# Block-masked attention and two MLPs: the score products of two heads side by side on 64 rows each

## The chip, the cores and the metric

The kernel runs on one core of one Trainium2 chip. The metric is the device time of one execution in microseconds (us), as the median of several runs. The profile is that of one further execution. Engines are named as in the profile: PE (matrix products), PEld (loading the stationary operand), DVE, ACT, POOL (elementwise engines), SP (the queue that issues all transfers here).

## The reference

```python
# q, k, v: (batch 4, heads 8, sequence 576, head_dim 64), float32
scores = scale * np.matmul(q, k.transpose(0, 1, 3, 2))
mask = block_i >= block_j                 # blocks of 64 positions
scores = np.where(mask, scores, -1000000000.0)
attn = np.exp(scores - max); attn = attn / (sum(attn) + 1e-09)
x = np.matmul(attn, v)                    # to (2304 tokens, 512)
h = x @ w_in;  g = h * np.cos(h);        x = g @ w_out      # MLP 1, width 2048
h = x @ w_in2; r = np.maximum(h, 0.0);   x = (r * r) @ w_out2   # MLP 2
```

MLP 1's weights come in as float64, all else as float32.

## The kernel before, in words

**Work and order.** The heads are taken in pairs, whose 2 x 64 dimensions fill the 128 partitions (TOP is the first head, BOT the second). Attention runs in 20 units: units 0 to 3 are batch 0, first 256 rows, for the four pairs; units 4 to 7 are batch 0, the other 320 rows; units 8 to 19 are whole pairs of batches 1 to 3. The first half of MLP 1 runs between them, group by group: tiles `h` (x times w_in) and `y` (times w_out). From about 400 us on only MLP work is left.

**The planner.** Nothing is issued as it is written. `Recorder` notes each operation with an estimated cost, the tiles it needs and a rank (its place in the list plus an offset per kind and phase, `PUT_OFF`, L36), and `schedule` then makes the order of every engine from these. Some copies may go to one of two engines by choice. Eight PSUM banks are shared by kind: `h` may hold 6, `y` 3, scores `s` 5, transposes `t` 3, products with v `a` 1, and one of each kind is kept free for it (`BANKS`, L22).

**Precision.** A float32 operand is split into a high and a low part (fp32r), and a product is three products: high by high, high by low, low by high.

**One unit, before.** `prep` (L856) transposes k and q of the pair on PE and makes the parts kh, kl (keys) and sa, sb (queries, scaled). From unit 4 on (`u.apart` false), the parts of one head are laid over both halves of the partitions: sa holds head 0's high part on its own half and its low part on the other half, sb the same for head 1. To match, six transfers through SP copy the halves of kh twice into ka and kb, and kl into the buffers kz, whose other half is zero (`both`, L866). Then two products over 128 rows, with ka and with kz, give the sum of the three. Units 0 to 3 do without copies: three products over the 64 rows of a head.

`unit_scores` (L926) runs per head and group of rows: rows 0 and 1 of 128 in one bank (128 and 256 keys), then row 3 (512 keys) and row 2 (384); a unit "P" computes the last 64 rows of both heads at once from `tails`. After the products come per row: `soft_min` on DVE (mask and row minimum), the exponential on ACT with its sum, the small add of 1e-9 (`eps`) and the reciprocal for the whole group, and the scaling on POOL (`times`). `unit_transpose` (L992) turns the result by PE and copies it out; `unit_av` (L1024) multiplies with v for one head. In units 0 to 7 (`u.plain`) v stays float32 and gives 64 output columns; from unit 8 on v's two parts fill 128 columns.

**Order in the list.** In the second part: head 0 row 3, head 0 row 2, P, product with v of head 0, `prep` of the next unit, head 1 row 3, row 2, product with v of head 1 (`UNITS` L1057, `attention` L1080).

Of the kernel before, what the change touches and what calls it, by code (L numbers as in the profile page):

```python
# [30 lines left out]
APART = 4  # L31
E1 = 7
# [313 lines left out]
def kernel(  # L346
# [264 lines left out]
    for i in range(2):  # L611
        sa = T(sb, [128, 512], F32R, f"sa{i}")
        sb_ = T(sb, [128, 512], F32R, f"sb{i}")
        tails = [T(sb, [128, 128], F32R, f"tail{i}{j}") for j in "hl"]
        for t in tails:
            memset(f(t), 0.0)

        pads = [T(sb, [128, 576], F32R, f"kz{i}{j}") for j in "ab"]
        memset(f(pads[0][64:128]), 0.0)
        memset(f(pads[1][0:64]), 0.0)  # L620
        QS.append((sa, sb_, tails, pads))
# [193 lines left out]
    def load_pair(b, p, part):  # L815
# [3 lines left out]
        u.apart = part == 1 or len(units) < APART  # L819
# [36 lines left out]
    def prep(u):  # L856

        kn, qn, vn = u.nat
        sa, sb_, tails, pads = u.S = QS[u.i % 2]
        ka, kb, kl, kh = u.K = tuple(T(sb, [128, 576], F32R, n, 2) for n in ("ka", "kb", "kl", "kh"))  # L860
# [5 lines left out]
        def both(which):  # L866
            if u.apart:
                return
            for i, h in enumerate((TOP, BOT)):
                if which == "h":  # L870
                    for g in (TOP, BOT):
                        dma(f(u.K[i][g]), f(kh[h]), 147456, 600.0)
                else:
                    dma(f(pads[i][h]), f(kl[h]), 147456, 600.0)

        def queries(t, c):
            if u.apart:

                act(sa[:, c], t, ACTF.Copy, scale=scale)
                stt(sb_[:, c], t, scale, f(sa[:, c]), ALU.mult, ALU.subtract)  # L880
                return
# [13 lines left out]
        else:  # L895
# [7 lines left out]
            both("h")  # L903
            lo_part(kl[:, 512:576], t[:, 0:64], kh[:, 512:576])
            both("l")
# [19 lines left out]
    @of("scores")  # L925
    def unit_scores(u, kind):  # L926

        e = T(sb, [128, 576], F32, "e", E1)
        st = T(sb, [128, 8], F32, "st", 6)
        if kind == "P":  # L930
            for j in range(2):
                t = bank("s")
                kc = slice(j * 288, j * 288 + 288)
                (th, tl), kl, kh = u.S[2], u.K[2][:, kc], u.K[3][:, kc]
                for i, (l, r) in enumerate(((th, kh), (th, kl), (tl, kh))):
                    matmul(t[:, 0:288], l, r, i == 0, i == 2, holds=(e, st))
                soft_min(e[:, kc], t[:, 0:288], mask[:, 0:288], st[:, 2 + j:3 + j])
            tt(st[:, 0:1], st[:, 2:3], st[:, 3:4], ALU.min)
            parts = [(0, 576)]
        else:  # L940
            h, ts_ = kind
            half = (TOP, BOT)[h]
            t = bank("s")
            parts, o = [], 0
            for j in ts_:
                n = 128 * (j + 1)
                c = slice(j * 128, j * 128 + 128)
                if u.apart:

                    (qh, ql), (kl, kh) = [x[half, c] for x in u.S[:2]], [x[half, 0:n] for x in u.K[2:]]  # L950
                    for i, (l, r) in enumerate(((qh, kh), (qh, kl), (ql, kh))):
                        matmul(t[:, o:o + n], l, r, i == 0, i == 2, holds=(e, st))
                else:

                    matmul(t[:, o:o + n], u.S[h][:, c], u.K[h][:, 0:n], True, False, holds=(e, st))
                    matmul(t[:, o:o + n], u.S[h][:, c], u.S[3][h][:, 0:n], False, True)
                parts.append((o, n))
                o += n
            for i, (o, n) in enumerate(parts):
                soft_min(e[:, o:o + n], t[:, o:o + n], mask[:, 512 - n:512], st[:, i:i + 1])  # L960
        for i, (o, n) in enumerate(parts):
            x = e[:, o:o + n]
            turn("exp", x, x, ACTF.Exp, bias=st[:, i:i + 1], scale=-1.0, accum_out=st[:, 4 + i:5 + i])
        m = len(parts)
        sums = st[:, 4:4 + m]
# [8 lines left out]
        rs = st[:, 6:6 + m]  # L974
        dve(75, lambda: nc.vector.reciprocal(real(rs), real(st[:, 4:4 + m])), [rs], [st[:, 4:4 + m]])  # L975
        for i, (o, n) in enumerate(parts):
            times(e[:, o:o + n], e[:, o:o + n], st[:, 6 + i:7 + i])
        return e

# [10 lines left out]

    @of("weighted")
    def unit_transpose(u, kind, e):  # L992

        names = "h" if u.plain else "hl"
        if kind == "P" or kind[1][0] > 0:
            if not hasattr(u, "r2"):
                u.r2 = [T(sb, [128, 2, 4, 320], F32R, f"r2{i}") for i in names]
                u.r2t = T(sb, [128, 2, 64], F32R, "r2t")
        t = t_tile()
        if kind == "P":  # L1000
            for kt in range(4):
                transpose(t[:, kt * 128:kt * 128 + 128], e[:, kt * 128:kt * 128 + 128], holds=u.r2)
            src = t.rearrange("p (k h c) -> p h k c", k=4, h=2)
            parts_of(u, src, [r[:, :, :, 256:320] for r in u.r2])
            t2 = t_tile()
            transpose(t2[0:64, 0:128], e[:, 512:576], holds=[u.r2t])
            parts_of(u, t2[0:64, 0:128].rearrange("p (h c) -> p h c", h=2), [u.r2t[0:64], u.r2t[64:128]])
            return
        h, ts_ = kind
        if ts_[0] == 0:  # L1010
            u.r1 = [T(sb, [128, 384], F32R, f"r1{i}", 2) for i in names]
            for o in (0, 128, 256):
                transpose(t[:, o:o + 128], e[:, o:o + 128], holds=u.r1)
            parts_of(u, t[:, 0:384], u.r1)
            return
        n = ts_[0] + 1
        for kt in range(n):
            transpose(t[:, kt * 128:kt * 128 + 128], e[:, kt * 128:kt * 128 + 128], holds=u.r2)
        o = (ts_[0] - 2) * 128
# [4 lines left out]
    def unit_av(u, h, region):  # L1024
# [4 lines left out]
        if region == 1:  # L1029
            mms = [(0, 256, 0, [r[:, 0:256] for r in u.r1]), (128, 256, 1, [r[:, 256:384] for r in u.r1])]  # L1030
        else:
            mms = []
            for kt in range(4):
                c = 128 if kt == 3 else 0
                mms.append((c, 320, kt, [r[:, h, kt, c:320] for r in u.r2]))

            mms.append((256, 320, 4, [u.r2t[:, h, :]]))
        mine, other = (TOP, BOT) if h == 0 else (BOT, TOP)
        mms = [(c0, c1, kt, r) for c0, c1, kt, rs in mms for r in rs]
        xb = None if u.plain else T(sb2, [128, 320], F32, "xb", 2)  # L1040
# [337 lines left out]
```

## Time and profile before

| | |
|---|---|
| Median of 3 runs | 1052.7 us (1052.44 to 1053.11) |
| Profiled execution, its own time | 1059.5 us |
| Its span, first to last instruction | 1057.7 us |
| Mean granted TensorE clock | 0.995 of full speed |
| PE busy | 1020.6 us |
| DVE, ACT, POOL busy | 698.7, 676.7, 376.7 us |
| Moved by DMA | 129.16 MB |

A matrix product's busy time in the profile includes its way through the array, so products overlap in it and a busy PE need not be a full one. What a product takes of PE in a dense run is the distance from its start to the next start.

### The profile page before, as it was taken

The numbers are of one execution on the slowest core, as the hardware profiler recorded it, in microseconds if no ns is written. First come the engines' busy times: TensorE is split into PE (matmuls) and PEld (weight loads), VectorE is DVE, ScalarE is ACT, GpSimd is POOL, SyncE is SP. The second block draws the span as 40 slices with busy tenths as digits, with TensorE's granted clock in tenths as the row PEclk, the third lists the DMA queues.
The fourth block names the chain that finished last, engine by engine and source line by source line (L and its number), as shares of the span: only waits on it lengthen the run. The fifth ranks groups of instructions, "written<-read, shape, count | busy, mean of one in ns | idle before, by whom it ended". The sixth has DMA issues, their size and how long they took to land.

```text
span 1057.7 us, 18891 instructions
## 1 busy us (share of the span) xinstructions
PE 1020.6 (96%) x6440; PEld 926.8 (88%) x6440; DVE 698.7 (66%) x1805; ACT 676.7 (64%) x1685; POOL 376.7 (36%) x466
## 2 busy tenths in 40 slices
PE   8959999999999999999999999999999999999998
PEld 5657788889899989999889999988989888988987
DVE  4687499886758674567653326999877287747433
ACT  5688689888979886776574336777755364524312
POOL 5336224454545556948982222114120002000000
PEclk9989999999999999999999999999999999999999
DMA  6686534534425124455321223375761383131121
GB/s 156 160 187 165 140 93 120 140 81 119 114 72 126 43 64 136 136 167 189 113 86 63 90 71 119 115 226 156 266 197 53 120 321 98 60 100 51 60 70 40
DMA packets 125919, 129.16 MB, mean 122 GB/s; under 512 B 72832, under 2 KB 99456, under 8 KB 124800
## 3 DMA queue, kind: packets, MB, share of 16 engines
q1 hardware_dynamic: 125824, 127.96, 41.2%
q8 instruction: 51, 0.84, 0.3%
q14 instruction: 44, 0.36, 0.1%
HBM read 81.79 MB, written 31.98 MB: 108 GB/s over the span
## 4 chain that ended last, share of the span: by engine, by line
PE 58%; ACT 12%; DVE 12%; POOL 9%; DMA 5%; issue 4%; SPq 0%; ACTq 0%; DVEq 0%; POOLq 0%
PE y L512 24%; PE h L512 23%; PE a L512 4%; PE t L521 3%; ACT e L397 3%; PE s L512 3%; POOL gl L450 3%; POOL c L691 2%; POOL w L450 2%; DVE e L918 1%; DVE c L413 1%; POOL xl L450 1%; ACT r2h L465 1%; DVE r L406 1%; DVE gl L454 1%
## 5 line engine op out<-in xcount | busy, mean ns | idle before, releaser
L512 PE MATMUL h<-xh,w 128*128 128x256 f32 (+1 forms) x1408 | 288.6, 298 | 0.6 <-ACT u L465 0.4
L512 PEld LDWEIGHTS h<-xh,w 128*128 128x128 f32 x1408 | 231.1, 188 | 4.2 <-ACT u L465 0.9
L512 PE MATMUL y<-gh,w 128*128 128x384 f32 (+2 forms) x896 | 218.3, 318 | 9.1 <-POOL w L431 7.5
L512 PE MATMUL h<-xl,w 128*128 128x256 f32 (+1 forms) x704 | 206.6, 294 | 0.3 <-POOL xl L450 0.3
L512 PE MATMUL y<-w,gh 128*128 128x512 f32 x576 | 182.2, 396 | 0.7 <-ACT gh L436 0.4
L512 PEld LDWEIGHTS y<-gh,w 128*128 128x128 f32 x896 | 156.4, 190 | 12.0 <-POOL w L431 7.7
L512 PE MATMUL y<-gl,w 128*128 128x384 f32 (+2 forms) x448 | 143.0, 321 | 3.3 <-POOL gl L450 3.1
L512 PEld LDWEIGHTS h<-xl,w 128*128 128x128 f32 x704 | 132.4, 188 | 1.4 <-POOL xl L450 0.6
L512 PEld LDWEIGHTS y<-w,gh 128*128 128x128 f32 x576 | 106.9, 187 | 27.1 <-ACT w L436 1.1
L450 POOL TENSOR_TENSOR gl<-r,gh 128x384 fp32r<-128x384 f32 (+2 forms) x95 | 91.1, 963 | 92.9 <-ACT gh L436 92.2
L436 ACT ACTIVATE gh<-r 128x256 fp32r<-128x256 f32 (+2 forms) x192 | 85.6, 446 | 45.4 <-DVE r L1291 30.9
L495 POOL TENSOR_SCALAR e<-e,st 128x128 f32<-128x128 f32 (+4 forms) x144 | 83.8, 592 | 86.2 <-DVE st L975 61.0
L512 PE MATMUL y<-w,gl 128*128 128x512 f32 x288 | 113.4, 395 | 0.2 <-DVE gl L454 0.2
L512 PEld LDWEIGHTS y<-gl,w 128*128 128x128 f32 x448 | 85.0, 190 | 7.3 <-POOL gl L450 6.2
L397 ACT ACTIVATE e<-e,st 128x128 f32<-128x128 f32 (+4 forms) x144 | 83.2, 579 | 10.1 <-DVE st L918 8.3
L406 DVE TENSOR_TENSOR r<-h,r 128x384 f32<-128x384 f32 (+2 forms) x112 | 55.7, 498 | 48.5 <-ACT r L397 48.3
L450 POOL TENSOR_TENSOR xl<-x,xh 128x384 fp32r<-128x384 f32 (+1 forms) x36 | 45.0, 1258 | 117.9 <-ACT xh L436 110.8
L413 DVE SCALAR_TENSOR_TENSOR r<-n,h 128x384 f32<-128x384 int32 (+2 forms) x112 | 55.1, 493 | 38.4 <-ACT n L397 26.5
L397 ACT ACTIVATE n<-h 128x384 int32<-128x384 f32 (+2 forms) x112 | 48.5, 437 | 48.6 <-PE h L512 47.5
L918 DVE CUSTOM_DVE_ANT_0 e<-s,mask 128x288 f32<-128x288 f32 (+4 forms) x160 | 73.1, 476 | 6.7 <-PE s L512 5.0
L521 PE MATMUL t<-ident,e 128*128 128x128 f32 (+1 forms) x400 | 70.7, 288 | 3.1 <-POOL e L495 2.6
L397 ACT ACTIVATE r<-r,halfpi 128x384 f32<-128x384 f32 (+2 forms) x112 | 63.4, 567 | 13.7 <-DVE r L413 13.0
(178 smaller groups left out, 2119.0 us busy)
## 6 DMA issues: line engine op xcount, KB each, us to landing
raw<-in_moe_w_in_dram SPq DMA_DIRECT2D x32, 512.0 KB, 4.3
raw<-in_moe_w_out_dram SPq DMA_DIRECT2D x32, 512.0 KB, 3.8
x<-y_d SPq DMA_DIRECT2D x32, 256.0 KB, 3.0
wi_d<-so SPq DMA_DIRECT2D x32, 256.0 KB, 3.3
w<-wi_d SPq DMA_DIRECT2D x8, 1024.0 KB, 7.5
k<-in_k_dram SPq DMA_DIRECT2D x36, 128.0 KB, 2.6
q<-in_q_dram SPq DMA_DIRECT2D x36, 128.0 KB, 2.7
v<-in_v_dram SPq DMA_DIRECT2D x36, 128.0 KB, 2.8
```

The costliest lines, as they stand in the source:

```text
L397: return nc.scalar.activation(real(out), real(in_), func, **kw)
L406: out.size / 0.96 + 68, lambda: nc.vector.tensor_tensor(real(out), real(a), real(b), op=op), [out], [a, b],
L413: lambda: nc.vector.scalar_tensor_tensor(real(out), real(a), s, real(b), op0=op0, op1=op1),
L436: "ACT": ("ACT", n / 1.2 + 92, lambda: nc.scalar.activation(real(hi), real(x), ACTF.Copy)),
L450: lambda: nc.gpsimd.tensor_tensor(real(lo), real(x), real(f(hi)), op=ALU.subtract), 1,
L454: lambda: nc.vector.tensor_tensor(real(lo), real(x), real(f(hi)), op=ALU.subtract), 1,
L465: "ACT": ("ACT", n / 1.2 + 50, lambda: nc.scalar.activation(real(out), real(ps), ACTF.Copy)),
L495: lambda: nc.gpsimd.tensor_scalar(real(out), real(x), real(s), 1.0, op0=ALU.mult, op1=ALU.mult),
L512: lambda: nc.tensor.matmul(real(ps), lhsT=real(lhsT), rhs=real(rhs), start=start, stop=stop, skip_group_check=True),
L521: lambda: nc.tensor.transpose(real(out), real(in_), real(ident)[0:rows, 0:rows]), [out], [in_, ident],
L691: lambda: nc.gpsimd.tensor_tensor(real(wi), real(t), real(wi), op=ALU.subtract), 1,
L918: lambda: nc.vector.tensor_tensor_reduce(out=real(e), in0=real(ps), in1=real(m), scale=-1.0, scalar=BIG, op0=ALU.add, op1=ALU.min, accum_o ...
```

## The change

The parts of one head no longer lie over both halves. All units now do what units 0 to 3 did (three products over the 64 rows of a head), but both heads of the pair are computed in one planner operation (`block`), alternating TOP and BOT, each head in a bank of its own. The copies ka, kb, kz and their six transfers per unit are gone; queries are made by one ACT and one DVE instruction over 128 partitions in place of two each over 64. `eps` and the reciprocal now run once for both heads of a block. In units 0 to 7 the product with v is a block too: the heads alternate between the two halves of the output, in one bank, and one copy of 128 partitions takes it out. The products with v of both heads come behind all transposes, and `prep` of the next unit comes just before them. The planner charges a score block 190 ns and each pair of products what one costs. The tiles r1 have 4 buffers in place of 2; score tiles `e` keep 7 and are taken two at a time.

```diff
+    def block(mms, cost, holds=()):
+        def fn():
+            for ps, l, r, start, stop in mms:
+                nc.tensor.matmul(real(ps), lhsT=real(l), rhs=real(r), start=start, stop=stop, skip_group_check=True)
+        R.op("PE", cost, fn, [m[0] for m in mms], [x for m in mms for x in m[1:3]], holds=holds)
...
-        pads = [T(sb, [128, 576], F32R, f"kz{i}{j}") for j in "ab"]
...
-        ka, kb, kl, kh = u.K = tuple(T(sb, [128, 576], F32R, n, 2) for n in ("ka", "kb", "kl", "kh"))
+        kh, kl = u.K = [T(sb, [128, 576], F32R, n, 2) for n in ("kh", "kl")]
...
-            for i, h in enumerate((TOP, BOT)):
-                if which == "h":
-                    for g in (TOP, BOT):
-                        dma(f(u.K[i][g]), f(kh[h]), 147456, 600.0)
-                else:
-                    dma(f(pads[i][h]), f(kl[h]), 147456, 600.0)
...
-            for s, h in ((sa, TOP), (sb_, BOT)):
-                act(s[h, c], t[h], ACTF.Copy, scale=scale)
-            for s, h, g in ((sa, TOP, BOT), (sb_, BOT, TOP)):
-                stt(s[g, c], t[h], scale, f(s[h, c]), ALU.mult, ALU.subtract)
+            act(sa[:, c], t, ACTF.Copy, scale=scale)
+            stt(sb_[:, c], t, scale, f(sa[:, c]), ALU.mult, ALU.subtract)
...
+    def unit_scores(u, rows):
+        es = [T(sb, [128, 576], F32, "e", E1) for _ in range(2)]
+        st = T(sb, [128, 12], F32, "st", 6)
+        ts_ = [bank("s") for _ in range(2)]
+        mms, parts, o, cost = [], [[], []], 0, 190
+        for j in rows:
+            n = 128 * (j + 1)
+            c = slice(j * 128, j * 128 + 128)
+            for i in range(3):
+                for h, half in enumerate((TOP, BOT)):
+                    q_, k_ = u.S[i == 2][half, c], u.K[i == 1][half, 0:n]
+                    mms.append((ts_[h][:, o:o + n], q_, k_, i == 0, i == 2))
+                cost += max(110.0, n / 2.2)
+            for h in range(2):
+                parts[h].append((h, o, n))
+            o += n
+        block(mms, cost, (*es, st, *ts_))
+        parts = parts[0] + parts[1]
+        for i, (h, o, n) in enumerate(parts):
+            soft_min(es[h][:, o:o + n], ts_[h][:, o:o + n], mask[:, 512 - n:512], st[:, i:i + 1])
+        normalized(st, [es[h][:, o:o + n] for h, o, n in parts])
...
         if u.plain:
+            a, mms, cost = bank("a"), [], 140
+            for i, (c0, c1, kt, rs) in enumerate(got):
+                rows = slice(0, 64) if kt == 4 else slice(0, 128)
+                cost += max(120.0, 4 * (c1 - c0) / 2.2)
+                for h, half in enumerate((TOP, BOT)):
+                    mms.append((a[half, c0:c1], u.nat[2][rows, kt, h], f(rs[h][0][rows]), i == 0, i == len(got) - 1))
+            block(mms, cost, [u.xt])
+            copy(u.xt[:, o:o + n], a[:, 0:n])
+            return
...
-            for kind, av in UNITS[r]:
-                e = unit_scores(u, kind)
-                unit_transpose(u, kind, e)
-                if av:
-                    unit_av(u, *av)
-                if kind == "P" or (u.part == 1 and av == (0, 1)):
-                    pair(i + 1)
-                    load(i + NATB)
+            for rows in [(0, 1)] if r == 1 else [(3,), (2,)]:
+                es = unit_scores(u, rows)
+                for h in range(2):
+                    unit_transpose(u, rows, h, es[h])
+            if r == 2:
+                last_transpose(u, last_scores(u))
+            if r == 2 or u.part == 1:
+                pair(i + 1)
+                load(i + NATB)
+            unit_av(u, r)
```

`last_scores` and `last_transpose` are the former P branches, and `normalized` the former end of `unit_scores`, with its work per part unchanged.

## Rows read from the trace of the kernel before

**Rows 1.** The page's part 4, chain that ended last, by engine.
```profile
PE 58%; ACT 12%; DVE 12%; POOL 9%; DMA 5%; issue 4%; SPq 0%; ACTq 0%; DVEq 0%; POOLq 0%
```
**Rows 2.** Busy time by stretch: length, PE, PEld, DVE, ACT, POOL, clock, DMA share, GB/s.
```profile
48.00:75.00 27.00, 15.85 (x96) 13.32 (x95) 25.08 (x60) 22.03 (x48) 7.02 (x10) 0.87 0.74 175
75.00:120.00 45.00, 44.57 (x268) 34.24 (x267) 34.49 (x105) 39.88 (x99) 26.57 (x31) 0.97 0.67 169
...
150.00:200.00 50.00, 46.70 (x332) 42.14 (x333) 46.78 (x163) 44.55 (x127) 22.38 (x37) 1.00 0.54 137
200.00:400.00 200.00, 193.49 (x1430) 184.11 (x1429) 145.84 (x463) 168.37 (x462) 97.41 (x147) 1.00 0.35 89
400.00:1058.00 658.00, 647.46 (x3956) 597.99 (x3954) 402.78 (x875) 353.96 (x830) 195.20 (x192) 1.00 0.38 124
```
**Rows 3.** Chain in order of time, 36 to 135 us: start, length, what.
```profile
52.08 5.97 DMA raw<-in_moe_w_in_dram
...
58.07 3.59 DMA k<-in_q_dram
...
80.73 2.34 PE a L512 x10
...
122.80 2.34 PE a L512 x10
```
**Rows 4.** SP's timeline, transfers issued around 52 us: start, length.
```profile
51.48 0.50 SPq L527 DMA_DIRECT2D ka<-kh  x1
...
55.16 0.60 SPq L527 DMA_DIRECT2D kz1b<-kl  x1
```
**Rows 5.** DMA issues by tensor, with size and time to landing.
```profile
ka<-kh SPq DMA_DIRECT2D x32, 144.0 KB, 2.6
```
**Rows 6.** PE's timeline, full-height score products: start, length, product.
```profile
217.14 0.28 PE L512 MATMUL s<-ka,sa 128*128 128x256 f32 x1
...
217.37 0.22 PE L512 MATMUL s<-kb,sb 128*128 128x128 f32 x1
...
217.54 0.34 PE L512 MATMUL s<-kb,sb 128*128 128x256 f32 x1
...
222.64 0.40 PE L512 MATMUL s<-kb,sb 128*128 128x512 f32 x1
...
223.11 0.40 PE L512 MATMUL y<-gh,w 128*128 128x256 f32 x2
```
**Rows 7.** PE's timeline, half-height score products of units 0 and 1.
```profile
7.42 0.47 PE L512 MATMUL s<-kh,sb 64*128 64x128 f32 x1
7.44 0.78 PE L512 MATMUL s<-kh,sa 64*128 64x128 f32 x2
...
8.67 0.51 PE L512 MATMUL s<-kh,sb 64*128 64x256 f32 x2
```
**Rows 8.** PE's timeline, half-height products of one head in sequence.
```profile
27.02 0.41 PE L512 MATMUL s<-kl,sa 64*128 64x256 f32 x1
27.24 0.41 PE L512 MATMUL s<-kh,sb 64*128 64x256 f32 x1
```
**Rows 9.** PE's timeline where full-height and half-height products meet.
```profile
37.56 0.28 PE L512 MATMUL h<-xs1h,w 128*128 128x256 f32 x1
37.77 0.33 PE L512 MATMUL s<-kh,sa 64*128 64x128 f32 x1
38.03 0.55 PE L521 MATMUL t<-ident,e 128*128 128x128 f32 x3
```
**Rows 10.** DVE by form, 0 to 400 us: busy us, mean ns, idle before.
```profile
L975 DVE RECIPROCAL st<-st 128x1 f32<-128x1 f32 x80 | 12.4, 157 | 4.6 <-ACT st L969 3.6
...
L413 DVE SCALAR_TENSOR_TENSOR sb<-t,sb 64x512 fp32r<-64x512 f32 x16 | 11.1, 693 | 1.7 <-ACT sb L397 1.2
```
**Rows 11.** ACT by form, 0 to 400 us.
```profile
L397 ACT ACTIVATE e<-e,st 128x512 f32<-128x512 f32 x32 | 23.0, 719 | 2.6 <-DVE st L918 2.4
...
L397 ACT ACTIVATE sa<-t 64x512 fp32r<-64x512 f32 x16 | 9.4, 586 | 1.9 <-PE t L521 1.7
```

More of the change, by code (lines that the diff above doesn't have):

```diff
@@ L30 @@
 PLAIN = 8
-APART = 4
 E1 = 7
@@ L818, in load_pair @@
         u.plain = len(units) < PLAIN
-        u.apart = part == 1 or len(units) < APART
         u.nat = []
@@ L923, in soft_min, with normalized @@
         )
[L925 to L962, printed above, removed]
+    def normalized(st, parts):
+        m = len(parts)
+        for i, x in enumerate(parts):
             turn("exp", x, x, ACTF.Exp, bias=st[:, i:i + 1], scale=-1.0, accum_out=st[:, 4 + i:5 + i])
-        m = len(parts)
-        sums = st[:, 4:4 + m]
+        sums, rs = st[:, 4:4 + m], st[:, 8:8 + m]
         flexible(
@@ new lines, in right_parts, with last_transpose @@
+    def right_parts(u):
+        if not hasattr(u, "r2"):
+            names = "h" if u.plain else "hl"
+            u.r2 = [T(sb, [128, 2, 4, 320], F32R, f"r2{i}") for i in names]
+            u.r2t = T(sb, [128, 2, 64], F32R, "r2t")
+    @of("weighted")
+    def last_transpose(u, e):
+        right_parts(u)
+        t = t_tile()
+        for kt in range(4):
+            transpose(t[:, kt * 128:kt * 128 + 128], e[:, kt * 128:kt * 128 + 128], holds=u.r2)
+        src = t.rearrange("p (k h c) -> p h k c", k=4, h=2)
+        parts_of(u, src, [r[:, :, :, 256:320] for r in u.r2])
+        t2 = t_tile()
+        transpose(t2[0:64, 0:128], e[:, 512:576], holds=[u.r2t])
+        parts_of(u, t2[0:64, 0:128].rearrange("p (h c) -> p h c", h=2), [u.r2t[0:64], u.r2t[64:128]])
@@ L1017, in unit_transpose @@
+    @of("weighted")
+    def unit_transpose(u, rows, h, e):
+        t = t_tile()
+        if rows[0] == 0:
+            r1 = [T(sb, [128, 384], F32R, f"r1{i}", 4) for i in ("h" if u.plain else "hl")]
+            u.r1[h] = r1
+            for o in (0, 128, 256):
+                transpose(t[:, o:o + 128], e[:, o:o + 128], holds=r1)
+            parts_of(u, t[:, 0:384], r1)
+            return
+        right_parts(u)
+        n = rows[0] + 1
         for kt in range(n):
             transpose(t[:, kt * 128:kt * 128 + 128], e[:, kt * 128:kt * 128 + 128], holds=u.r2)
-        o = (ts_[0] - 2) * 128
+        o = (rows[0] - 2) * 128
@@ L1037, in unit_av @@
[L1037 to L1040, printed above, removed]
-        for i, (c0, c1, kt, r) in enumerate(mms):
-            first, last = i == 0, i == len(mms) - 1
-            if u.plain:
-                rows = slice(0, 64) if kt == 4 else slice(0, 128)
-                matmul(a[mine, c0:c1], u.nat[2][rows, kt, h], f(r[rows]), first, last, holds=[u.xt], passes=4)
-            else:
-                matmul(a[:, c0:c1], u.vs[:, kt, h].rearrange("p s d -> p (s d)"), r, first, last, holds=(xb, u.xt))
+                got.append((c, 320, kt, [[r[:, h, kt, c:320] for r in u.r2] for h in range(2)]))
@@ L1048, in unit_av @@
+            got.append((256, 320, 4, [[u.r2t[:, h, :]] for h in range(2)]))
         n, o = (256, 0) if region == 1 else (320, 256)
         if u.plain:
-            copy(u.xt[mine, o:o + n], a[mine, 0:n])
-        else:
+            a, mms, cost = bank("a"), [], 140
[4 more added lines that the diff above has]
+                    mms.append((a[half, c0:c1], u.nat[2][rows, kt, h], f(rs[h][0][rows]), i == 0, i == len(got) - 1))
@@ new lines, in unit_av @@
+            block(mms, cost, [u.xt])
+            copy(u.xt[:, o:o + n], a[:, 0:n])
+            return
+        xb = T(sb2, [128, 320], F32, "xb", 2)
+        for h, (mine, other) in enumerate(((TOP, BOT), (BOT, TOP))):
+            a = bank("a")
+            mms = [(c0, c1, kt, r) for c0, c1, kt, rs in got for r in rs[h]]
+            for i, (c0, c1, kt, r) in enumerate(mms):
+                vs = u.vs[:, kt, h].rearrange("p s d -> p (s d)")
+                matmul(a[:, c0:c1], vs, r, i == 0, i == len(mms) - 1, holds=(xb, u.xt))
```

73 lines of the change are left out of this document (26 added, 47 removed).

## The prediction

> **What bounds the kernel now.** I read the chain of waits first. PE holds 58% of it, ACT and DVE 12% each, DMA 5% [rows 1]: PE is the usual bound, but not everywhere. The table by stretch shows where. Behind 400 us there is only MLP work, 658 us that the change does not touch [rows 2]. From 48 to 75 us PE is busy 15.85 of 27 us while DVE is busy 25.08 and the DMA engines 74%: weights and keys come in and are split, and PE waits. From 75 to 120 us PE is busy all the time, but ACT is at 39.88 of 45. From 150 to 200 us DVE is at 46.78 of 50, above PE's 46.70; from 200 to 400 us PE is at 193.49 of 200 and ACT at 168.37 [rows 2]. The chain in order of time names the pieces: a weight transfer of 5.97 us at 52.08, a transfer of q at 58.07, and then eight stretches of ten products with v, 2.34 us each, from 80.73 to 125.14 [rows 3]. Those eight are units 4 to 7, two heads each, and all lie on the chain. PE's timeline gives what a product takes from start to start.
>
> **Score products.** Before, a head and row group is two full-height products. Start to start, such a pair takes 0.23 us at 256 columns (217.14 to 217.37), 0.17 at 128 (217.37 to 217.54), 0.47 at 512 (222.64 to 223.11) [rows 6]; for 384 I take 0.35, midway. Both heads of a whole unit: 2 x (0.17 + 0.23 + 0.35 + 0.47) = 2.44 us. After, there are six half-height products per row group, 6 x 1280 = 7680 columns in a unit; at 2.4 GHz, one after another, 3.2 us. Whether the two halves run side by side decides. Units 0 and 1 show it: at 7.42 and 7.44 us two products on different halves start 0.02 us apart [rows 7]. In that stretch of ten rows 13 products (seven of 128 columns and six of 256, 2432 columns) start from 7.42 us on; the last row holds two and ends at 9.18, so at 0.41 us each [rows 8] the last starts at 8.77, and its 128 columns take 0.11 more: 1.45 us in all. The clock was at its lower level there, since products of one half that follow each other start 0.22 us apart at 256 columns, that is 1.2 GHz [rows 8]; 2432 columns one after another are 2.03 us. So the overlap is at least 1.4, in a stretch whose halves were unevenly filled; two is the most. I take 1.7: 1.88 us. Each block also meets full-height work at both ends: from the `h` product at 37.56 to the score product at 37.77 are 0.21 us where 0.12 is usual, and that product of 128 columns holds PE for 0.26 until the transpose at 38.03 [rows 9], where a full-height one takes 0.09, half of its pair's 0.17. That is 0.09 and 0.17 more; I take 0.24 us a block, three blocks a unit: 0.72. Sum 2.60 us against 2.44: 0.16 us more in each of 12 whole units and about 0.1 in units 4 to 7, together 2 us more on PE. The bounds: overlap of 2 gives 2.32, 1.4 gives 3.0, none 3.92.
>
> The Trainium skill (TensorE: Matmul & The Clock Gate, Part 3, Measured speedup vs the span model) says that products on different row groups cost one product's time plus about 4 ns each. By that rule the block would come to 2.32 us and the sum to about 4 us less; the starts 0.02 us apart agree, the 1.45 us do so only in part.
>
> **Products with v in units 0 to 7.** Each head now takes 2.34 us in units 4 to 7 [rows 3]. If the two halves of the output run side by side, four of the eight stretches go: 9.4 us. No row shows two such products at once, so the gain lies between 0 and 9.4. The nearest row is the overlap of the two row halves [rows 7], so I take the upper end for PE. Then ACT comes next: it loses in the four units 4 x 0.59 us of queries [rows 11], about four `eps` of 0.2, and four of the eight copies of the product (0.4 each, estimated from 0.59 at 512 columns): 4.8 of 39.88 us. At the same share of the stretch (0.886) 35.1 us of ACT need 39.6 us in place of 45. I take 6 us, between that 5.4 and 9.4. In units 0 to 3 the same happens on a smaller scale, but ends in the stretch from 48 us that PE does not set; I count 1 us.
>
> The Trainium skill (the same page and part, What overlaps and what doesn't) says that a load overlaps running products only where row groups differ, and these pairs share all rows; the same part's table gives a speedup of 2.38 for three column groups of 32. An estimate from that table, two thirds of it, 1.59, would make the 9.4 us into 6.9. No run so far shows it.
>
> **Transfers.** 96 copies of 144 KB go (32 of ka, 32 of kb, 32 of kz) [rows 5], 14 of 129 MB. What matters is SP's order: from 51.48 to 55.76 us it issued six copies, 3.4 us, around the weight transfer of 52.08 and ahead of the loads of k and q, for one of which the chain waits at 58.07 [rows 3, 4]. They come up to 3.4 us earlier; everything behind a copy also stops waiting for kh and kl, which the copy waited for. Bounds 0 and 3.4, and the next lateness is DVE's, at 25.08 of 27 us [rows 2]. I take the upper end, 3.4, since the copies stood directly ahead of the load on the chain. Later the copies are hidden behind MLP products and I count nothing; without that cover a unit would gain one landing, 2.6 us.
>
> **DVE and ACT.** 16 units lose one query subtraction (0.69 us of DVE [rows 10]) and one query copy (0.59 us of ACT [rows 11]); the remaining one works on 512 columns too, so I give it the same time. A whole unit has three fewer reciprocals (3 x 0.157 us [rows 10]) and three fewer `eps`, of like size, shared by both engines: 1.4 us of DVE and 0.9 of ACT. In 135 to 200 us, where DVE sets the pace, four units save at most 5.6 us; I take 4. From 200 to 400 us PE sets it, and eight units save 7 us of ACT beside the work on PE; I take 2.5.
>
> **Moved and waiting.** `prep` of the next unit (nine transposes, its copies and queries) now stands behind head 1's rows in the list, past their score products; its transfers are gone, so SP sees nothing new. I cost it at nothing: the MLP products fill PE meanwhile; without that cover about 3 us a unit (nine transposes of 0.11, 0.59 and 0.69 for the queries, as much for the keys). Four r1 buffers cost nothing on any engine.
>
> **Sum.** Up to 75 us 3.4 + 1 = 4.4; 75 to 135 us 6; 135 to 400 us 4 + 2.5 - 2 = 4.5. Together 15 us off the profiled execution's 1059.5 us: 1044.5. The median of the runs is 0.9936 of that execution, so 1038 us.
>
> **Rivals.**
> 1. *Output halves do not run side by side.* For it: no row shows them so, and they load on the same rows. Against: the row halves do overlap [rows 7]. It takes back the 6 and the 1, while the fewer ACT copies still give some 0.5: 8.5 us off the execution, 1044 us.
> 2. *Hidden anyway.* Units were planned around MLP products; what PE, DVE and ACT lose in work they wait in other places. For it: from 200 to 400 us no engine but PE is near full [rows 2]. Only the 3.4 us of SP and some 2 more remain, less 2 of the blocks' ends and 2 lost elsewhere: about 1051.5 us.
> 3. *Late normalisation; slower.* `eps` and the reciprocal now wait for the exponentials of both heads. Head 0's scaling on POOL, its transposes and products are late by head 1's exponentials: 0.72 us in row 3 [rows 11], by its columns 0.54 each in row 2 and in rows 0 and 1; the shorter ones cost more by the column, so I take 2.5 us a unit. Behind POOL's scaling PE's transposes wait, and behind those, in PE's order, MLP products that could run. Fully exposed in 12 units it is 30 us; six tenths of it 18, against 15 gained: 3 us over the execution of before, 1056 us. It decides from 15 us, half of it exposed. Against it: the planner knows these waits and can put MLP products first.
> 4. *Row halves run one after another at full clock; slower.* 3.92 in place of 2.44 us, 12 x 1.48 + 4 x 1.1 = 22 us more on PE, in place of the 2 counted: 1059.5 + 5 = 1064.5, as a median 1058 us. Against it stand the starts 0.02 us apart [rows 7].
>
> **Chances.** Forecast 0.57, output halves apart 0.13, hidden 0.07, late normalisation 0.15, row halves apart 0.08. Predicted is the forecast, 1038 us; its own range is 1028 to 1048 (the overlap's bounds, 4 us less and 5 more, and ACT's or PE's bound in units 4 to 7). For 8 in 10 the range takes in rivals 1 and 2 and about half of rival 3: 1027 to 1057. A difference under 0.2% (2 us) cannot be told from no change here; by the cases faster has 0.72, same 0.06, slower 0.22.
>
> **What would show it.** Right: pairs of half-height score products starting some 0.02 us apart at each block, a block of row 3 near 0.9 us; two products with v starting together, and about 2.4 us for both heads; no ka, kb, kz; shorter stretches before 135 us; an unchanged 650 us of MLP at the end. Wrong: score products evenly spaced, PE waiting for POOL's scaling (rival 3), or the stretch from 135 to 400 us grown.

## The result and the profile after

| | before | after |
|---|---|---|
| Median of 4 runs each, same chip | 1052.9 us (1052.44 to 1053.58) | 1043.3 us (1042.15 to 1044.06) |
| Ratio | | 0.9907 (95%: 0.989 to 0.9925) |
| Profiled execution, its own time | 1059.5 us | 1044.06 us |
| Span, mean granted clock | 1057.7 us, 0.995 | 1042.3 us, 0.986 |
| PE, DVE, ACT, POOL busy | 1020.6, 698.7, 676.7, 376.7 us | 1002.6, 675.7, 660.9, 362.6 us |
| Moved by DMA | 129.16 MB | 115.00 MB |

The change is faster by 0.93%, 9.6 us in medians; 1038 us was forecast, with a range of its own of 1028 to 1048. The two profiled executions lie 15.4 us apart. Which of the two differences is the gain takes a section of its own further down.

The chain of waits by engine, after:

```profile
PE 68%; POOL 10%; DVE 7%; ACT 7%; DMA 4%; issue 2%; SPq 1%; POOLq 0%; DVEq 0%; ACTq 0%
```

DVE and ACT have given up 10 points of the chain to PE [rows 1]. The table by stretch, with the columns of [rows 2]:

```profile
48.00:75.00 27.00, 19.05 (x115) 16.32 (x113) 21.04 (x53) 21.46 (x47) 14.34 (x15) 0.81 0.44 126
75.00:120.00 45.00, 42.54 (x312) 32.74 (x312) 25.21 (x83) 32.59 (x84) 16.00 (x21) 0.96 0.44 109
...
150.00:200.00 50.00, 48.41 (x378) 43.99 (x379) 42.96 (x136) 42.97 (x120) 24.52 (x42) 1.00 0.28 73
200.00:400.00 200.00, 198.98 (x1549) 186.03 (x1547) 137.32 (x420) 164.15 (x444) 102.08 (x148) 1.00 0.24 64
```

From 150 to 400 us PE is now the one bound: it is busy 48.41 of 50 and then 198.98 of 200 us, and DVE, which stood above it from 150 to 200, has fallen from 46.78 to 42.96. From 75 to 120 us it is the other way round: ACT has dropped from 39.88 to 32.59, further than the 35.1 of the forecast, but PE, busy 44.57 of 45 us before, now idles for 2.46. The chain in order of time says why; first its pieces, then SP's timeline beside them:

```profile
76.11 2.38 PE a L521 x20
78.50 0.38 SPq L534
...
81.82 4.40 DMA raw<-in_moe_w_out_dram
...
92.19 4.04 PE a L521 x20
...
105.02 2.35 PE a L521 x20
...
114.74 2.38 PE a L521 x20
```

```profile
78.50 3.21 SPq L534 DMA_DIRECT2D v<-in_v_dram  x4
81.82 0.53 SPq L672 DMA_DIRECT2D raw<-in_moe_w_out_dram  x1
```

Where the chain of before had eight stretches of 2.34 us, there are four, each for both heads: 2.38, 4.04, 2.35, 2.38. But from 78.50 on the chain leaves PE: four loads of v wait at the head of SP's queue until the products at 76.11 have freed v's one buffer, take 3.21 us to issue, and behind them comes the weight transfer of 4.40 us that the MLP needs. PE returns to the chain at 90.62. From 85 to 92 us it is busy only 4.69 of 7 us, at a granted clock of 1.00; from 92 to 97 the clock is 0.66, so the second block takes 4.04 where the others take 2.36.

The last block with v of units 0 to 3, after:

```profile
38.57 0.87 PE L521 MATMUL a<-r1h,v 128*64 128x256 f32 x8
```

From its end to the end of the last block of units 4 to 7 are 77.7 us (39.44 to 117.12). Before, the same stretch took 77.6 (47.52 to 125.14). The blocks do shorten it: from the start of the first of units 4 to 7 to the end of the last are 41.1 us (76.04 to 117.12), where there were 44.5 (80.66 to 125.14). But the first comes 36.6 us behind units 0 to 3 in place of 33.1.

PE's timeline for a block of row 3 at full clock, with the product before it and after it:

```profile
220.51 0.40 PE L511 MATMUL a<-r2h,vs 128*128 128x320 f32 x1
220.83 0.50 PE L521 MATMUL s<-kh,sa 64*128 64x512 f32 x2
221.17 0.40 PE L521 MATMUL s<-kl,sa 64*128 64x512 f32 x2
221.41 0.39 PE L521 MATMUL s<-kh,sb 64*128 64x512 f32 x2
221.73 0.41 PE L511 MATMUL a<-r2l,vs 128*128 128x320 f32 x1
221.98 0.31 PE L511 MATMUL a<-r2h,vs 128*128 128x320 f32 x1
222.13 0.31 PE L511 MATMUL a<-r2l,vs 128*128 128x320 f32 x1
```

Each line of `x2` is one product for either head; the two start 2 to 5 ns apart in the trace. From the first start to what follows the block, 0.90 us (220.83 to 221.73). The full-height product ahead of it takes 0.32 (220.51 to 220.83) where its like takes 0.15 (221.98 to 222.13): that is the price of the change from full to half height. The same for a block with v:

```profile
104.95 2.16 PE L521 MATMUL a<-r2h,v 128*64 128x320 f32 x16
107.04 0.33 PE L521 MATMUL a<-r2t,v 64*64 64x64 f32 x4
```

The small work, DVE first and then ACT, by form, 0 to 400 us:

```profile
L412 DVE SCALAR_TENSOR_TENSOR sb<-t,sa 128x512 fp32r<-128x512 f32 x16 | 11.0, 687 | 0.8 <-ACT sa L396 0.5
...
L396 ACT ACTIVATE sa<-t 128x512 fp32r<-128x512 f32 x16 | 9.6, 599 | 0.3
```

A query operation over 128 partitions takes what one over 64 took (687 against 693 ns, 599 against 586 [rows 10, 11]), and there are half as many.

### The profile page after: what moved, and what is told of

Same layout as the page of the kernel before. It is cut to its first block, busy times and chain, and to the rows that moved or that the text cites. A ratio compares the mean times of both kernels' runs of the same rounds, so it can differ in the third digit from the quotient of the medians.

```text
span 1042.3 us, 18745 instructions
## 1 busy us (share of the span) xinstructions
PE 1002.6 (96%) x6552; PEld 909.8 (87%) x6552; DVE 675.7 (65%) x1720; ACT 660.9 (63%) x1643; POOL 362.6 (35%) x453
## 2 busy tenths in 40 slices
DMA packets 118238, 115.00 MB, mean 110 GB/s; under 512 B 71296, under 2 KB 97920, under 8 KB 117120
## 4 chain that ended last, share of the span: by engine, by line
PE 68%; POOL 10%; DVE 7%; ACT 7%; DMA 4%; issue 2%; SPq 1%; POOLq 0%; DVEq 0%; ACTq 0%
PE y L511 29%; PE h L511 28%; PE t L528 4%; PE a L511 3%; POOL gl L449 3%; DMA raw<-in_moe_w_in_dram 2%; PE s L521 2%; POOL w L449 2%; POOL c L694 2%; DVE c L412 1%; PE a L521 1%; ACT e L396 1%; ACT t L396 1%; PE s L511 1%; DMA raw<-in_moe_w_out_dram 1%
## 5 line engine op out<-in xcount | busy, mean ns | idle before, releaser
L511 PE MATMUL y<-gh,w 128*128 128x384 f32 (+2 forms) x896 | 222.4, 324 | 9.6 <-POOL w L430 3.7
L901 DVE CUSTOM_DVE_ANT_0 e<-s,mask 128x384 f32<-128x384 f32 (+4 forms) x160 | 71.7, 476 | 12.7 <-PE s L511 7.4
L449 POOL TENSOR_TENSOR xl<-x,xh 128x384 fp32r<-128x384 f32 (+1 forms) x34 | 38.0, 1124 | 120.1 <-ACT xh L435 113.0
L528 PE MATMUL t<-ident,e 128*128 128x128 f32 (+1 forms) x400 | 67.7, 289 | 6.1 <-POOL e L494 5.7
```

Of the source, the lines that this page charges most:

```text
L449: lambda: nc.gpsimd.tensor_tensor(real(lo), real(x), real(f(hi)), op=ALU.subtract), 1,
L511: lambda: nc.tensor.matmul(real(ps), lhsT=real(lhsT), rhs=real(rhs), start=start, stop=stop, skip_group_check=True),
L901: lambda: nc.vector.tensor_tensor_reduce(out=real(e), in0=real(ps), in1=real(m), scale=-1.0, scalar=BIG, op0=ALU.add, op1=ALU.min, accum_o ...
```

## The experiments

Edits are against the kernel after unless "before" is said. The kernel after was not run again beside them; two of them, *e1_scores_serial* and *e6_copies_unread*, came out at its time in their own sessions (1043.4 both).

**Score products, head after head.**

```diff
             o += n
+        mms = mms[0::2] + mms[1::2]
         block(mms, cost, (*es, st, *ts_))
```

> The changed kernel with the products of each score block issued head after head in place of alternating; same plan, same work. Theory of the sum (PE sets the pace from 200 to 400 us and the overlap keeps the score blocks at the old cost): 1.3 to 1.5 us more on PE in each of 12 whole units and about 1 us in units 4 to 7, so 12 to 22 us over the changed kernel's 1043.3: 1055 to 1065. Rival (the PE time of the scores is covered by waits that stay): under 4 us more, 1043 to 1047.

Measured: 1043.4 us (1041.6 to 1044.7, 6 runs), no difference. PE's timeline of a block of row 3:

```profile
53.67 0.51 PE L521 MATMUL s<-kh,sa 64*128 64x512 f32 x2
54.01 0.40 PE L521 MATMUL s<-kl,sa 64*128 64x512 f32 x2
54.24 0.40 PE L521 MATMUL s<-kh,sb 64*128 64x512 f32 x2
```

In the program PE's instructions are now kh, kl, kh of one head and then the same of the other, and still they start in pairs, 10 to 17 ns apart. So the edit did not take the overlap away here. In the block of rows 0 and 1, where each head has six products, it did in part:

```profile
200.19 0.32 PE L521 MATMUL s<-kh,sa 64*128 64x128 f32 x1
...
200.48 0.43 PE L521 MATMUL s<-kh,sa 64*128 64x128 f32 x2
...
201.36 0.33 PE L528 MATMUL t<-ident,k 128*128 128x128 f32 x1
```

The other head starts 0.28 us behind, and the block takes 1.17 us (200.19 to 201.36), where the alternating one takes 0.89. Counted from the starts behind 60 us, the score blocks take 39.9 us here and 36.3 in the kernel after. So some 3.6 us of PE are lost without any difference in time; the granted clock is a little higher (0.991 as a median against 0.9885), which may hide them. The run prices neither the overlap nor its loss in full. It shows that alternating the heads is not what makes the row halves overlap where each head has three products.

**Products with v, head after head.** The same line in `unit_av`, ahead of its `block`.

> The changed kernel with the products with v of units 0 to 7 issued head after head in place of alternating. Theory of the sum: the 9.4 us of PE in units 4 to 7 come back, 7 us of them on the path: 1049 to 1052. Rival (the stretch from 48 to 117 us is set by the weights that come in and are split, since it lasted 77.7 us before and after): under 3 us, 1043 to 1046.

Measured: 1050.3 us (1049.5 to 1052.1, 6 runs), 7.0 more. PE's timeline:

```profile
73.75 2.15 PE L521 MATMUL a<-r2h,v 128*64 128x320 f32 x8
75.83 0.33 PE L521 MATMUL a<-r2t,v 64*64 64x64 f32 x2
76.09 2.15 PE L521 MATMUL a<-r2h,v 128*64 128x320 f32 x8
```

One head takes 2.34 us (73.75 to 76.09), then the other; the block that alternates takes 2.35 for both. Here alternating is everything, and the overlap of the two output halves is worth 7 us.

**Before, with no copies.** Units 4 to 19 take the three half-height products that units 0 to 3 take, each still an operation of its own for the planner.

```diff
-APART = 4
+APART = 99
```

> The kernel before with all units as units 0 to 3 had it: no copies, three half-height products per head and row group, heads not paired, products with v per head, sums per head. Theory of the sum: transfers, DVE and ACT give some 10 us as in the change, the products without overlap take back 22 us of PE: 1058 to 1068. Rival (the copies and the wait for their landing were what the change removed; the overlap hardly matters): 1040 to 1048.

Measured: 1121.2 us (1115.8 to 1123.8, 6 runs), far above what was expected.

**Before, with each head's products in one operation.** The same, but the products of one head and row group go into one `block`; heads are not paired.

```diff
-                    for i, (l, r) in enumerate(((qh, kh), (qh, kl), (ql, kh))):
-                        matmul(t[:, o:o + n], l, r, i == 0, i == 2, holds=(e, st))
...
+                for i, (l, r) in enumerate(((qh, kh), (qh, kl), (ql, kh))):
+                    mms.append((t[:, o:o + n], l, r, i == 0, i == 2))
+                    cost += max(110.0, n / 2.2)
...
+            block(mms, cost, (e, st, t))
```

> The kernel before without copies as in the earlier run, but with the three or six half-height products of one head and row group in one planner operation; heads still not paired. It tells standing together from pairing. If the overlap of the heads is what pays: 3.9 us of products and twice as many block ends, 5.3 us a unit in place of 2.44, 35 us more on PE, 1070 to 1085. If standing together pays and overlap does not: 1045 to 1055, at most 12 us more for block ends.

Measured: 1083.1 us (1079.8 to 1084.5, 4 runs). Its row 3, one head:

```profile
220.06 0.50 PE L522 MATMUL s<-kh,sa 64*128 64x512 f32 x1
220.40 0.39 PE L522 MATMUL s<-kl,sa 64*128 64x512 f32 x1
220.63 0.39 PE L522 MATMUL s<-kh,sb 64*128 64x512 f32 x1
220.95 0.66 PE L529 MATMUL t<-ident,q 128*128 128x128 f32 x4
```

One head takes 0.89 us (220.06 to 220.95); in the kernel after, both take 0.90. So the row halves overlap in full. A whole unit would pay its 2.52 us of blocks twice, about 30 us in 12 whole units and a smaller sum in units 4 to 7; the run lies 40 above the kernel after, which also has the products with v in blocks. Between this kernel and the one with separate operations lie 38 us. Counted from the trace, half-height score products stand in 140 separate runs there, in 87 here, in 47 in the kernel after. The table by stretch shows another part; first with separate operations, then with one per head:

```profile
300.00:350.00 50.00, 50.00 (x318) 44.94 (x317) 23.80 (x71) 29.71 (x81) 17.41 (x25) 0.88 0.19 51
350.00:400.00 50.00, 49.56 (x295) 41.15 (x295) 28.27 (x97) 32.77 (x97) 17.39 (x27) 0.86 0.20 54
400.00:450.00 50.00, 49.45 (x240) 39.33 (x239) 28.60 (x96) 34.08 (x98) 21.33 (x34) 0.76 0.03 10
```

```profile
300.00:350.00 50.00, 49.79 (x352) 44.31 (x351) 30.45 (x105) 36.98 (x107) 21.07 (x34) 1.00 0.19 50
350.00:400.00 50.00, 49.84 (x347) 44.72 (x346) 30.20 (x101) 37.01 (x105) 22.63 (x33) 1.00 0.15 42
```

PE is busy nearly all the time in both, yet with the half-height products spread out the granted clock is 0.88, 0.86 and 0.76 in three stretches: 0.12, 0.14 and 0.24 of 50 us each, 25 us of full clock lost. So most of the 38 us go with the clock; the changes between heights are what is left to explain the rest. In the 7 us ahead of each of the three falls (at 298, 360 and 421 us) PE is busy 6.51, 6.56 and 6.52 us. That spreading lowers the clock was not tried by itself.

**Before, with only the products with v in blocks,** in units 4 to 7:

```diff
+        if u.plain and region == 2:
+            return both_av(u, h)
```

(`both_av` is the block of `unit_av` after, run at the second head.)

> The kernel before with one part of the change alone: in units 4 to 7 both heads' products with v in one alternating block behind both heads' transposes, one copy out; scores, copies and queries as before. Theory of the sum: 6 us less, 1045 to 1049. Rival (the weights set that stretch): within 2 us of 1052.8.

Measured: 1048.4 us as a median (five runs from 1045.3 to 1048.6, one 1057.5, of which there is no profile).

**The kernel before again,** unchanged, for a second profile.

> The kernel before, unchanged, for a second profile. In its first profile (1059.5 us) the first rise of the granted clock came 37 us after the start, in the profiles of the four runs so far at 18 to 21 us, one of them with the same first units. Theory (the two levels of this kernel, 1052 to 1056 and 1060 to 1065 us, are an early and a late first rise): a run near 1052 has its rise at about 20 us and its last product with v of units 0 to 3 at about 40 us in place of 47.2; a run near 1061 has both late. Rival (the level is made elsewhere): the two do not go together.

Measured: 1061.9 us, span 1060.1. More on it below.

**The copies back, unread.** Six transfers a unit as before, into tiles that nobody reads:

```diff
+            both("h")
             lo_part(kl[:, 512:576], t[:, 0:64], kh[:, 512:576])
+            both("l")
```

> The changed kernel with the six transfers per unit put back at their old place in the list, into tiles that nobody reads. Theory of the sum (the transfers cost by their place in SP's order and their load): 3 to 5 us more than 1043.3. Rival (only the wait of the scores for the landed copies, or DVE and ACT, counted): within 1 us of 1043.3.

Measured: 1043.4 us (1041.5 to 1046.5, 4 runs), no difference. In the order of the kernel after, then, the copies cost nothing by being issued; the wait of the scores for landed copies is not in this run.

**Queries by halves.** From unit 4 on, two ACT and two DVE operations of 64 partitions, with the same values:

```diff
-            act(sa[:, c], t, ACTF.Copy, scale=scale)
-            stt(sb_[:, c], t, scale, f(sa[:, c]), ALU.mult, ALU.subtract)
+            for g in (slice(0, 128),) if u.i < 4 else (TOP, BOT):
+                act(sa[g, c], t[g], ACTF.Copy, scale=scale)
+            for g in (slice(0, 128),) if u.i < 4 else (TOP, BOT):
+                stt(sb_[g, c], t[g], scale, f(sa[g, c]), ALU.mult, ALU.subtract)
```

> The changed kernel with the query parts made by two ACT and two DVE instructions over 64 partitions each again, from unit 4 on. Theory of the sum (0.69 us of DVE and 0.59 of ACT a unit count where DVE and PE set the pace): 3 to 6 us more than 1043.3. Rival (both engines have room): within 1 us.

Measured: 1053.7 us (1051.7 to 1056.9, 12 runs), 10.4 more. DVE by form, 0 to 400 us:

```profile
L412 DVE SCALAR_TENSOR_TENSOR sb<-t,sa 64x512 fp32r<-64x512 f32 x32 | 22.0, 688 | 6.9 <-ACT sa L396 6.4
```

16 more operations are 11.0 us of DVE, and as many of 0.6 us on ACT; in idle time of DVE ahead of them 6.1 us more. All of that lies before 400 us, and the time grew by about as much as DVE's own work. These operations are not hidden. But not all of the 10.4 us is their own time: the granted clock is 0.985 as a median against 0.9885, which is some 4 us of full clock, and from 48 to 75 us it is 0.71 in this profile, where it was 0.81.

**Sums per head.** `eps` and reciprocal for each head by itself, as before the change:

```diff
-        normalized(st, [es[h][:, o:o + n] for h, o, n in parts])
+        m = len(parts) // 2
+        for g in range(2):
+            normalized(st, [es[h][:, o:o + n] for h, o, n in parts[g * m:g * m + m]], g * m)
```

> The changed kernel with the small add and the reciprocal once per head again (two of each per block in place of one), so that head 0's scaling does not wait for head 1's exponentials; products, copies and queries as changed. Rival 3 (late normalisation takes back part of the gain): 3 to 8 us less than 1043.3. Theory of the sum (the fewer small instructions are a gain, the lateness is covered): 1 to 4 us more.

Measured: 1039.0 us (1037.3 to 1040.0, 6 runs), 4.3 less. PE's transposes behind POOL's scaling, 12 to 40 us (us in total, times, longest), in the kernel after and then here:

```profile
PE t L528 <- POOL e L494: 5.4, 5, 3.0
```

```profile
PE t L528 <- POOL e L494: 2.4, 4, 0.9
```

This is the wait that rival 3 names, in units 0 to 3. The kernel before has none of it in this stretch, nor has the one with only v's products in blocks, which has the same units 0 to 3. With sums per head the last product with v of units 0 to 3 ends at 35.78 us in place of 39.44, 3.7 us earlier. Of this lead 1.3 us are left where units 4 to 7 start theirs (74.73 against 76.04); it is 4.6 where they end them, and 5.5 at the end of the two profiles. Behind 40 us the same wait is longer here (4.5 us in place of some 0.3, up to 400 us). So the wait is there and sums per head shorten it where no other work fills PE, but the planner makes another order from other operations, and how much of the 4.3 us is this wait is open.

**Preparation early.** `prep` and the load of the next unit ahead of row 2's transposes:

```diff
                 es = unit_scores(u, rows)
+                if rows == (2,):
+                    pair(i + 1)
+                    load(i + NATB)
```

> The changed kernel with the preparation of the next pair behind the scores of row 2 in the list, ahead of its transposes and of P, nearer to its old place. If its move behind all transposes made the next unit's scores late: 2 to 6 us less than 1043.3. If it is covered, as the forecast had it: within 2 us.

Measured: 1041.1 us (1039.7 to 1044.1, 6 runs), 2.2 less. The chain in order of time, 70 to 118 us, holds neither SP nor DMA any more, and the second block runs at full clock:

```profile
76.11 2.35 PE a L521 x20
...
92.92 2.35 PE a L521 x20
```

What has not changed is SP's queue:

```profile
78.50 2.79 SPq L534 DMA_DIRECT2D v<-in_v_dram  x4
81.40 0.53 SPq L672 DMA_DIRECT2D raw<-in_moe_w_out_dram  x1
```

The loads of v still wait for their buffer until 78.50, and the weight transfer leaves 0.42 us earlier at 81.40. So it is not the end of that wait that brings the 2.2 us; PE has other work meanwhile, and is busy 5.47 us from 85 to 92 where it was 4.69. At 2.2 us, in another session, the difference is hardly more than what can be told from none.

**Two buffers for v's loads.** `NATB = 2` in place of 1.

> The changed kernel with two buffers in place of one for each of k, q and v, so that the next loads do not wait for the products with v, which now come last in a unit. In the changed kernel's chain a load of v follows a product with v by way of SP at 78.5, 117.1 and 122.8 us. If that is the wait which took the place of the PE time saved in units 4 to 7: 3 to 8 us less than 1043.3. If the weights set that stretch: within 2 us.

Measured: 1047.6 us (1045.8 to 1049.5, 6 runs), 4.3 more, the wrong way for anyone who thinks that the wait for v's buffer is the loss. Two loads in advance change the order in SP's queue as well, and the granted clock is the lowest of the kernels built on after (0.982 as a median, some 7 us of full clock below after's 0.9885); which part costs is open.

**Sums per head and preparation early.** Both edits.

> The changed kernel with both mends that were faster alone: sums and reciprocals per head (1039.0) and the preparation of the next pair behind the scores of row 2 (1041.1). If they take away two separate waits their 4.3 and 2.2 us add up: 1036 to 1038. If both shorten the same wait (scores and scaling of the next block late): 1038 to 1040. If the order alone makes the difference from plan to plan: anywhere from 1037 to 1045.

Measured: 1038.8 us (1036.9 to 1039.6, 6 runs), 0.9831 of before (95%: 0.9792 to 0.987, over both of before's levels, below). It beats the kernels before and after, but sums per head alone do as well; the two do not add.

## The two levels of the kernel before

In the sessions of the experiments the kernel before ran 50 times beside them, at two levels: 18 runs from 1052.2 to 1055.7 us, 32 from 1059.6 to 1064.9, with nothing between. The runs of the result were all at the lower one, and both of its profiles (1059.5, 1061.9) are at the higher. The kernel after has one level, 1041.5 to 1046.5 with the runs that equal it.

The medians of the two levels, 1053.0 and 1061.6, lie 8.6 us apart. One other kernel helps to see where they are: up to unit 3 the one with only v's products in blocks has the code of the kernel before. From 20 to 30 us, in the two profiles of before and then in that one (columns of [rows 2]):

```profile
20.00:30.00 10.00, 10.00 (x31) 5.88 (x30) 5.00 (x16) 6.26 (x16) 3.41 (x7) 1.00 0.29 82
```

```profile
20.00:30.00 10.00, 10.00 (x31) 5.89 (x30) 5.00 (x14) 6.39 (x16) 3.42 (x7) 1.00 0.29 84
```

```profile
20.00:30.00 10.00, 10.00 (x57) 6.70 (x57) 9.04 (x29) 9.34 (x29) 6.12 (x11) 1.00 0.67 177
```

31 products against 57, with PE busy all the time. The clock column gives 1.00 for all three and does not show it; the distances do. In the profiles of before, products of 256 columns follow each other at 0.22 us in this stretch [rows 8]; in the other kernel:

```profile
23.84 0.28 PE L512 MATMUL s<-kl,sa 64*128 64x256 f32 x1
23.96 0.27 PE L512 MATMUL s<-kh,sb 64*128 64x256 f32 x1
```

0.12 us, the higher of the two clock levels. The rise comes at about 37 us in both profiles of before, between 11.6 and 22.5 us in every other one. By the last products with v in units 0 to 3 the difference has become 7.5 us, first before, then the other kernel:

```profile
46.66 0.86 PE L512 MATMUL a<-r1h,v 128*64 128x256 f32 x4
```

```profile
39.20 0.86 PE L512 MATMUL a<-r1h,v 128*64 128x256 f32 x4
```

That is most of the distance of the two levels. No profile of the kernel before at the lower level was taken, so that its shorter runs rise early is argued from this neighbour, not shown. If it is so, of the 15.4 us between the two profiled executions some 6 to 7 are the late rise, and the change itself is worth the 9.6 of the medians; against the median of the higher level it would be about 18.

## Why the prediction was right, and where it was off

The direction held, both overlaps that the forecast rests on are there, and the time is 5 us above 1038. But several terms missed, and the gain does not lie where the sum has it, so that the total came so near is in part luck. By its steps:

- **Where the gain lies.** The sum had 4.4 us up to 75 us, 6 from there to 135 and 4.5 behind. In the two profiles, after is 4.6 us ahead at the first product with v of units 4 to 7 (76.04 against 80.66), 8.0 at the end of the last (117.12 against 125.14), 18.0 at the last product with v of all (381.39 against 399.42) and 15.4 at the end. The kernel before with only v's products in blocks, which rises early and has the code of before up to there, is at the first of these places at 76.02. So the 4.6 us are the late rise, as far as this neighbour shows it, and the change brought nothing where 4.4 were forecast, then 3.4 in place of 6, then 10.0 in place of 4.5, of which the MLP work gave 2.6 back. How this divides against a run of before at the lower level is not measured.
- **Score blocks, "together 2 us more on PE".** The blocks of the unit at 216 us take 0.89, 0.90 and 0.73 us, 2.52 from the first start to what follows; with some 0.1 to 0.17 at each entry about 2.9, where 2.60 was forecast. The overlap is full, not 1.7 (0.90 for both heads, 0.89 for one); the entries cost more. But the full-height products of before were under-counted too: over units 4 to 19, counted from the starts in both traces, 45.4 us before, 40.4 after plus about 4 at the entries. A wash, as the step said within 3 us. The rule of the Trainium skill that the prediction weighed (TensorE: Matmul & The Clock Gate, Part 3, Measured speedup vs the span model) agrees with the pair's own time. Rival 4 is out.
- **Products with v, 6 + 1 us.** Undoing the overlap costs 7.0. In the kernel before the pairs alone bring about 4 (1048.4 against some 1052.7). One head takes 2.34 us and both take 2.35, so the estimate of 1.59 for two such halves was too low, and rival 1 is out. In the two profiles units 4 to 7 are 3.4 us shorter (44.5 to 41.1), where 6 were forecast; 1.7 of the rest is the second block at the lower clock.
- **Transfers, 3.4 us.** Failed: with the copies back the time is the same, and the first product with v of units 4 to 7 starts at 76.04 us without copies and at 76.02 in the kernel before with only v's products in blocks, which has them. That they stood directly ahead of a load on the chain of one execution was not enough, and the lower bound, 0, held. What was late next in their place was not tried apart.
- **DVE and ACT, 4 + 2.5 us.** Too small: to take back the queries alone costs 10.4, of which up to 4 go with the clock, in another order of the planner.
- **Preparation at nothing, and rival 3.** Not nothing: 4.3 us come back when the sums are per head, 2.2 (hardly beyond what can be told) when `prep` and the load stand earlier, not more with both. Rival 3's wait is there: PE waits 5.4 us for POOL's scaling in units 0 to 3, where the kernel before does not wait at all. It is far from the rival's 18, and not where the rival looked for it, in the 12 whole units. Rival 2 is out as a whole by the 9.6 us, though the 3.6 us of PE that *e1_scores_serial* adds without a later end suggest that a few us can hide.
- **The MLP unchanged.** From the start of the long run of `y` behind POOL's last piece in the chain (550.86 us before, 530.50 after) to the end of the span are 506.8 us before and 511.8 after. It was not quite untouched: 5 us of a lead of 20.4 are given back. About one is that after has 3054 products left at that point and before 3046. Most of the rest is the clock, which falls at 529 us, amid 2.7 us in which PE waits for POOL and ACT. The long run of `y` in the chain, before and after, and then a stretch of after (columns of [rows 2]):

```profile
550.86 12.40 PE y L512 x70
```

```profile
530.50 14.59 PE y L511 x68
```

```profile
532.00:536.00 4.00, 4.00 (x14) 4.00 (x14) 0.56 (x1) 1.15 (x3) 1.60 (x2) 0.50 0.28 88
```

- **The granted clock, which has no term in the sum.** Its mean is about 0.995 in the runs of before at either level (the time ahead of the first rise counts as 1.00 there) and 0.986 to 0.990 in those of after. As an estimate from these shares and the spans, after is at the lower level for some 7 us of full clock more. Not all of it is on the path: with the copies back it is 0.9845 at the same time. Two pieces are: the second block with v (1.7 us) and the run of `y` above.
- **"The median of the runs is 0.9936 of that execution, so 1038 us."** The sum, 15 us off the profiled execution, gave 1044.5, and after's profiled execution took 1044.06. This looks better than it is: the 6.8 us between execution and median were, as argued above, one late rise, which after's execution does not have, so part of those 15.4 us is not the change's. Taken off the median of before, as the prediction in effect did, 15 us were too many by 5.4: 3.4 of transfers that cost nothing, and what the late normalisation, `prep` and the clock take back, less what the queries gave beyond their term. These terms do not add to better than a few us, since each edit gives the planner another order.

## What to carry to other kernels

Where two halves of the array can work for two independent products, the gain is full when the products stand together: alternate them by hand, always where only the output halves differ, and keep all half-height work of a row group in one run. An operation that serves two heads at once makes the first head wait for the second: look at the place where nothing else fills the matrix engine, here the first units. When a profiled execution stands off the median of the runs, find the place of the difference before scaling a sum by it. A wait that the chain shows need not be the price: the loads of v wait for their buffer in the faster kernel too, and with two buffers the time grew. Compare the granted clock of two runs before a small difference is put down to an edit.

## What the runs showed of the hardware

- **Row halves overlap across the program's order, to a degree.** With the heads one after the other in the program, three products each, products of the second head start 10 to 17 ns behind those of the first; with six each the second head starts 0.28 us behind, and the block takes 1.17 us in place of 0.89. The Trainium skill (TensorE: Matmul & The Clock Gate, Part 3, What overlaps and what doesn't) says that products start strictly in the program's order; these starts differ. Output halves over the same rows do not do this: 2.34 us for each head in sequence, 2.35 for both when alternated.
- **Changing from full to half height** prolongs the product before by 0.09 to 0.17 us (0.21 in place of 0.12 [rows 9], 0.32 in place of 0.15, the two places shown).
- **The clock can fall with PE busy almost throughout.** 0.76 from 400 to 450 us with PE busy 49.45 of 50, where single half-height products were spread among full-height ones (6.52 of 7 us ahead of the fall); 1.00 from 300 to 400 us where they stood in blocks, against 0.88 and 0.86. That the spreading is the cause is not shown.
- **One program, two levels.** 8.6 us of 1053 between the medians; in the profiles at the higher level PE's pace first rises at 37 us, while the clock column says 1.00 ahead of it. That the lower level rises early is argued, not shown.
